# A spectral filter and MLP on one core: the remainder products of the last 64 features taken as 64-row products, two steps' side by side in TensorE's row halves

## The chip, the core and the metric

The kernel runs on one core of a Trainium2 chip. The core has TensorE (PE in the profile; its loads of stationary operands are shown apart, as PEld), VectorE (DVE), ScalarE (ACT), GpSimd (POOL) and SyncE (SP, which here issues nearly all DMAs). The metric is the device time of one execution in microseconds; before the change it is 1029.7 us, the median of three runs (1028.49 to 1030.01).

## The reference

Two residual blocks over 2048 tokens of 576 features, all in float32. The first is a spectral filter, the second an MLP with a ReLU between its two layers:

```python
h = x + irfft2(rfft2(layernorm(x)) * (w_r + 1j * w_i))
h2 = h + maximum(layernorm(h) @ w1, 0) @ w2      # w1: 576 x 4608, w2: 4608 x 576
```

## The kernel before

The program is one hand-ordered list of instructions for each engine; what is written first in the code runs first on its engine.

**Three stretches.** Up to about 100 us the tokens are normalized and transformed (lines 258 to 399). Then comes the inverse transform, in a loop `u` (line 739) which for two token tiles at a time also does the second normalization (`stat2`, `norm2`) and the transposition of the normalized tile (`project`, line 505), and which starts the first steps of the MLP (`unit`). From about 200 us on only the MLP runs.

**Two numbers for each.** Products run on data of the type float32r. Operands are split in two of that type, a high part (the rounded value, written by ScalarE) and a low part or remainder (value minus high part). A product of two matrices is three products: high by high, high by low, low by high.

**The MLP's steps.** The 4608 hidden features are taken in 18 groups `g` of 256, the tokens in four chunks `c` of 512; a step is one pair (g, c), 72 in all, listed in `steps` (line 727). From step 8 (`WINO`) on the order is group by group, chunks 0, 1, 2, 3 in each, so that neighbouring steps have neighbouring chunks, the last chunk of a group being followed by the first of the next.

**The transposed tokens.** `xc[c]` holds a chunk transposed: features on the 128 partitions, 512 tokens along the row, in nine blocks. Blocks 0 to 3 are the high parts of features 0 to 511, blocks 5 to 8 their low parts. Block 4 holds the last 64 features, 512 to 575, twice: on partitions 64 to 127 the high part, on partitions 0 to 63 the low part. `project` makes it: the last transpose (line 510) takes features 448 to 575, so that the last 64 land in the upper partitions; one ScalarE copy of 640 columns writes blocks 0 to 4 (line 514), another 512 plain columns for GpSimd's subtraction, and VectorE writes the low part into the lower half (line 520).

**The first layer** is `mm1(i, a, part)` (line 525): for step i and half a of its 256 hidden features, a sum over 14 products of 128 rows and 512 columns. Blocks 0 to 3 give three each; block 4 gives two, with the high weights (times high and low part at once, since the weights of the last 64 features are loaded in both partition halves) and with the low weights. From step 9 on the sum is cut in two parts of seven products; the four (a, part) are the step's quarters 0 to 3.

**The second layer** in those steps is a scheme with seven block products instead of eight (`prod`, line 620), each of six products of 288 columns. `slot(i)` (line 655) runs step i's seven block products and between them the four quarters of step i+1's first layer: quarter 0, A11·B11 and A12·B21, quarter 1, S2·T2 and S1·T1, quarter 2, S3·T3 and S4·B22, quarter 3, A22·T4. After quarters 1 and 3 ScalarE, VectorE and GpSimd take the ReLU, the splits and the sums of the hidden values (`hid_a`, line 607), which later block products read. The sums of the first layer lie in two PSUM tiles, one for each a, with one bank for even and one for odd steps (`hid_p`, line 604).

**Weights.** `load_weights` (line 306) loads a group's weights five steps ahead of its first step. `split_weights` (line 325) queues their split in pieces; for the first layer there are five, one for each block, and `work(1)` in the slots of chunks 1 and 2 takes the next piece from the queue: three in the slot of chunk 1, two in that of chunk 2.

Of the kernel before, what the change touches and what calls it, by code (L numbers as in the profile page):

```python
# [21 lines left out]
GF = 2  # L22
NG = DFF // (128 * GF)
CH = 4
# [104 lines left out]
def kernel(ctx: ExitStack, tc: tile.TileContext, x, w_r, w_i, w1, w2, cc2, c1, fb, ib, c3, out):  # L129
    nc = tc.nc  # L130
# [3 lines left out]
    def sb(shape, tag, bufs=1, dt=F32):  # L134
        n[0] += 1
        return pool.tile(shape, dt, tag=tag, name=f"{tag}_{n[0]}", bufs=bufs)
# [3 lines left out]
    def ps():  # L140
        n[0] += 1
        return psum.tile([128, 1024], F32, tag="d", name=f"d_{n[0]}", bufs=4)

    def ebuf(shape, dt=F32):
        e = sb([128, EW], "e", EB, dt)[:, :int(np.prod(shape[1:]))]
        return e.rearrange("p (a b) -> p a b", a=shape[1]) if len(shape) == 3 else e

    def mm(o, l, r, start, stop):
        nc.tensor.matmul(o, l, r, start=start, stop=stop)  # L149

    def act(o, i, **kw):
        nc.scalar.activation(o, i, AF.Copy, **kw)  # L152
# [9 lines left out]
    ident = sb([128, 128], "ident")  # L162
# [141 lines left out]
    raw, wts = {}, {}  # L304
# [16 lines left out]
    def work(k):  # L321
        for _ in range(k):
            split(*pieces.pop(0))

    def split_weights(g, part):
        if g == 1 and part == 0:
            h, l = tail[0][:, 4608:5888], tail[0][:, 5888:7168]
        else:
            h, l = (ebuf([128, (1280, 1152)[part]], F32R) for _ in range(2))
        h, l = (v.rearrange("p (a n) -> p a n", a=(5, 2)[part]) for v in (h, l))  # L330
        wts[g, part] = h, l
        for k in range((5, 2)[part]) if g >= 2 else [slice(None)]:
            pieces.append((h[:, k], l[:, k], raw[g][part][:, k]))
        if g <= 2:
            work(len(pieces))
# [63 lines left out]
    for i in range(NP + 2):  # L399
        if i < NP:  # L400
            if i % 2 == 0:
                mid_l(i, i + 1)
            mid_d(i)
        if i == NP - 3:
            load_weights(0)
        if 1 <= i <= NP:
            mid_b(i - 1)
        if i >= NP:
            split_weights(0, i - NP)
        if i >= 2:  # L410
            if i > NP:
                warm_pe(8)
            mid_i(i - 2)
# [16 lines left out]
    xc = [xc01[:, 0], xc01[:, 1], xc2]  # L430
# [74 lines left out]
    def project(t):  # L505
        y = Zs.pop(t)
        pz = ps()
        for b in range(4):
            nc.tensor.transpose(pz[:, 128 * b:128 * b + 128], y[:, 128 * b:128 * b + 128], ident)  # L509
        nc.tensor.transpose(pz[:, 512:640], y[:, 448:576], ident)  # L510
        q = slice(128 * (t % CH), 128 * (t % CH) + 128)
        dst = xc[t // CH]
        pzv = pz.rearrange("p (a s) -> p a s", s=128)
        act(dst[:, 0:5, q], pzv[:, :5])
        if t % 2 == 0:
            Ez[t] = ebuf([128, 1024])
        zt = Ez[t - t % 2][:, 512 * (t % 2):512 * (t % 2) + 512]
        act(zt, pz[:, :512])
        nc.gpsimd.tensor_sub(dst[:, 5:9, q], zt.rearrange("p (a s) -> p a s", s=128), dst[:, 0:4, q])
        nc.vector.tensor_sub(dst[0:64, 4, q], pzv[64:128, 4], dst[64:128, 4, q])  # L520

    hid = {}
    pend = {}

    def mm1(i, a, part=None):
        g, c = steps[i]
        w1h, w1l = wts[g, 0]
        if a == 0 and not part:
            pend[i] = None if i >= WINO else ps()
        p = hid_p(i, a) if i >= WINO else pend[i][:, 512 * a:512 * a + 512]  # L530
        f = slice(128 * a, 128 * a + 128)
        ops = []
        for kt in range(4):
            ops += [(w1h, kt, kt), (w1h, kt, 5 + kt), (w1l, kt, kt)]
        ops += [(w1h, 4, 4), (w1l, 4, 4)]
        for n_, (w, kt, xk) in enumerate(ops):
            if part is None or n_ // 7 == part:
                mm(p, w[:, kt, f], xc[c][:, xk, :], n_ == 0, n_ == len(ops) - 1)
        if i >= WINO:
            return  # L540
        if a == GF - 1:
            p = pend.pop(i).rearrange("p (a s) -> p a s", a=GF)
            hh, hl = sb([128, GF, 512], "D", 4, F32R), sb([128, GF, 512], "D", 4, F32R)
            nc.scalar.activation(hh, p, AF.Relu)  # L544
            nc.vector.scalar_tensor_tensor(hl, p, 0.0, hh, op0=ALU.max, op1=ALU.subtract)  # L545
            hid[i] = (hh, hl)
# [21 lines left out]
    WINO = 8  # L568
# [35 lines left out]
    def hid_p(i, k):  # L604
        return wps[2 + k][:, 512 * (i % 2):512 * (i % 2) + 512]
# [49 lines left out]
    def slot(i):  # L655
# [4 lines left out]
        def quarter(k):  # L660
            mm1(i + 1, k // 2, k % 2)
            if k % 2 and end:
                for hs in range(2):
                    relu_split(fs[f"A{hs + 1}{k // 2 + 1}"], hid_p(i + 1, k // 2)[:, 256 * hs:256 * hs + 256])
            elif k % 2:
                hid_a(i + 1, k // 2)
# [60 lines left out]
    steps = first + [(g, c) for g in range(2, NG) for c in range(NC)]  # L727

    def unit(k):
        i, q = divmod(k, 4)  # L730
        if q < 2:
            mm1(i, q)
        else:
            if i == 2:
                mm1(3, q - 2)
            mm2(i, 2 * q - 4)
            mm2(i, 2 * q - 3)

    for u in range(NT // 2 + 3):
        if u <= NT // 2:  # L740
            inv_h(u, u != 1)
        if 2 * u < NT:
            inv_d(2 * u)
            inv_d(2 * u + 1)
        if u == 1:
            inv_r(u)
        if u == 7:
            load_weights(1)
        if u == 8:
            tail.append(sb([128, 10240], "X", dt=F32R))  # L750
            xc.append(tail[0][:, :4608].rearrange("p (a n) -> p a n", a=9))
        if 3 <= u:
            project(2 * u - 6)
            project(2 * u - 5)
        if 1 <= u <= NT // 2:
            stat2(2 * u - 2)
            stat2(2 * u - 1)
        if 2 <= u < NT // 2 + 2:
            for _ in norm2(2 * u - 4, 2):
                pass  # L760
        if u in (8, 9):
            split_weights(1, u - 8)
        if 5 <= u:
            unit(2 * u - 10)
            unit(2 * u - 9)
    for i in range(3, len(steps)):
        if i + 5 < len(steps) and steps[i + 5] == (steps[i + 5][0], 0):
            load_weights(steps[i + 5][0])
        if i + 3 < len(steps) and steps[i + 3] == (steps[i + 3][0], 0):
            split_weights(steps[i + 3][0], 0)  # L770
        if i == WINO - 3:
            wino_sums(2, 1, 2, 3, 4)
        if i == WINO - 2:
            wino_w("B11", "B21", "T2", "T1", "T3")
        if i == WINO - 1:
            wps += [None, None, ps(), ps()]
            wino_tiles()
        if i == WINO:
            wps[:2] = ps(), ps()
        if i >= WINO:  # L780
            (slot if i + 1 < len(steps) else slot_last)(i)
            continue
        for a in range(GF):
            mm1(i + 1, a)
            if i == WINO - 1:
                hid_a(i + 1, a)
        for tt in range(CH):
            mm2(i, tt)
        if i == WINO - 1:
            relu_split(fs["A22"], hid_p(i + 1, 1)[:, 256:])  # L790
            split(*fs["S3f"], fs["S3"])
            wino_w("B22", "T4")
# [22 lines left out]
```

## Time and profile before

| | us |
|---|---|
| median of three runs | 1029.7 |
| span of the profiled execution | 1026.5 |
| PE busy | 1011.1 |
| DVE busy | 741.4 |
| ACT busy | 391.1 |
| POOL busy | 326.0 |

The profile shows one execution. Its span runs from the first to the last instruction; the 3.2 us between it and the median of the runs lie around it. A row of a timeline has the start, the length from the first start to the last end, the engine, the line, the operation, out<-in by the program's names with the buffer numbers left out, for a product the rows and columns of PE's array that it uses (128*128, 64*64), then partitions x elements of the operand, and the count; a bracket holds the idle time before it and who ended it. Neighbouring products overlap, since the end of one is modelled with the time that its result needs to come out: the time that one takes is read from start to start. The chain of waits is the work that ended last, followed backwards and listed in order of time.

### The profile page before, as it was taken

What the parts mean: (1) busy time and instruction counts of PE and PEld (TensorE: products, weight loads), DVE (VectorE), ACT (ScalarE), POOL (GpSimd) and SP (SyncE); (2) the same over time, 40 slices, a digit from 0 to 9 for tenths busy, and PEclk for the clock granted to TensorE, in tenths of its full rate; (3) what the DMA queues carried; (4) which work ended last, traced back from release to release, by engine and by line L of the source; (5) the groups of instructions that cost most, each with busy time, mean ns of one, the idle gap of its engine ahead of it and who ended that gap; (6) DMA issues with size and microseconds to landing.
All of it is one profiled execution on the core that took longest, in us unless ns stands there. A gap on an engine that the chain in (4) does not pass through costs nothing.

```text
span 1026.5 us, 17863 instructions
## 1 busy us (share of the span) xinstructions
PE 1011.1 (98%) x6894; PEld 899.2 (88%) x6894; DVE 741.4 (72%) x1366; ACT 391.1 (38%) x891; POOL 326.0 (32%) x429
## 2 busy tenths in 40 slices
PE   7999999999999999999999999999999999999997
PEld 6877678899999999999999999999999999999997
DVE  7689877334678777777777777877777777777774
ACT  5645354311233343343334343334334333334331
POOL 4201465110233333323232433333332323243321
PEclk7999999999999999999999999999999999999999
DMA  9944500110000000000110000000000011000024
GB/s 243 219 129 115 121 21 30 49 38 13 27 24 27 25 27 24 27 24 27 33 41 27 24 27 24 27 24 26 24 27 24 26 33 41 27 24 1 1 59 127
DMA packets 32101, 48.01 MB, mean 47 GB/s; under 512 B 2960, under 2 KB 22800, under 8 KB 32016
## 3 DMA queue, kind: packets, MB, share of 16 engines
q1 hardware_dynamic: 31280, 45.98, 16.7%
q8 instruction: 55, 0.90, 0.4%
q10 hardware_dynamic: 736, 0.89, 0.3%
q14 instruction: 30, 0.25, 0.1%
HBM read 42.13 MB, written 4.72 MB: 46 GB/s over the span
## 4 chain that ended last, share of the span: by engine, by line
PE 94%; DVE 3%; DMA 2%; SPq 0%; ACT 0%; issue 0%; DVEq 0%; ACTq 0%
PE d L149 58%; PE d L627 35%; DMA A<-in_A_x_dram 2%; DVE st L209 1%; PE d L509 1%; DMA X<-in_A_x_dram 0%; DVE A L469 0%; DVE D L545 0%; DVE e L253 0%; DVE mv L210 0%; ACT D L544 0%; DVE e L252 0%; DVE e L488 0%; SPq L424 0%; SPq L160 0%
## 5 line engine op out<-in xcount | busy, mean ns | idle before, releaser
L634 DVE TENSOR_TENSOR A<-A,d 128x576 f32<-128x576 f32 x445 | 332.5, 747 | 51.2 <-PE d L627 51.0
L627 PE MATMUL d<-X,D 128*128 128x288 f32 x2286 | 342.8, 294 | 0.0
L627 PEld LDWEIGHTS d<-X,D 128*128 128x128 f32 x2286 | 326.4, 188 | 14.7
L149 PE MATMUL d<-B,e 128*128 128x512 f32 x952 | 237.4, 390 | 0.0
L149 PEld LDWEIGHTS d<-B,e 128*128 128x128 f32 x952 | 171.9, 188 | 27.9 <-issue 0.2
L602 DVE SCALAR_TENSOR_TENSOR D<-d,D 128x256 fp32r<-128x256 f32 x191 | 81.1, 425 | 121.8 <-ACT D L601 121.8
L601 ACT ACTIVATE D<-d 128x256 fp32r<-128x256 f32 x191 | 73.0, 382 | 242.3 <-PE d L149 242.3
L616 POOL TENSOR_TENSOR e<-e 128x256 f32<-128x256 f32 x63 | 46.6, 740 | 350.0 <-ACT e L615 350.0
L149 PE MATMUL d<-C,e 128*128 128x512 f32 x476 | 119.0, 390 | 0.0
L149 PE MATMUL d<-X,e 128*128 128x512 f32 x476 | 118.8, 390 | 0.0
L152 ACT ACTIVATE X<-e 128x288 fp32r<-128x288 f32 (+2 forms) x176 | 69.8, 434 | 103.5 <-PE d L627 103.5
L317 DVE TENSOR_TENSOR D<-e,D 128x512 fp32r<-128x512 f32 x126 | 91.2, 724 | 19.5 <-ACT D L152 19.5
L612 POOL TENSOR_TENSOR e<-e 128x256 f32<-128x256 f32 x63 | 46.8, 744 | 170.1 <-ACT e L611 170.1
L149 PEld LDWEIGHTS d<-C,e 128*128 128x128 f32 x476 | 85.9, 188 | 13.8
L149 PEld LDWEIGHTS d<-X,e 128*128 128x128 f32 x476 | 85.9, 188 | 13.7
L152 ACT ACTIVATE D<-e 128x512 fp32r<-128x512 f32 x126 | 65.6, 521 | 73.7 <-POOL e L617 70.2
L317 DVE TENSOR_TENSOR X<-e,X 128x288 fp32r<-128x288 f32 (+2 forms) x176 | 82.8, 493 | 0.3 <-POOL r L212 0.3
L627 PEld LDWEIGHTS d<-X 128*128 128x128 f32 x378 | 57.2, 188 | 4.9
L627 PE MATMUL d<-X 128*128 128x288 f32 x378 | 60.4, 295 | 0.0
L149 PE MATMUL d<-e,D 128*128 128x288 f32 x384 | 52.7, 296 | 0.0
L149 PEld LDWEIGHTS d<-e,D 128*128 128x128 f32 x384 | 51.9, 189 | 0.7 <-ACT e L152 0.2
L617 POOL TENSOR_TENSOR e<-e,e 128x256 f32<-128x256 f32 x63 | 49.7, 790 | 4.9
(86 smaller groups left out, 938.0 us busy)
## 6 DMA issues: line engine op xcount, KB each, us to landing
e<-in_B_w_dram SPq DMA_DIRECT2D x18, 576.0 KB, 4.0
e<-in_B_w_dram SPq DMA_DIRECT2D x18, 512.0 KB, 3.7
A<-in_A_x_dram SPq DMA_DIRECT2D x16, 288.0 KB, 8.7
out_dram<-A SPq DMA_DIRECT2D x28, 144.0 KB, 2.5
X<-in_A_x_dram SPq DMA_DIRECT2D x12, 288.0 KB, 7.4
e<-in_B_w_dram SPq DMA_DIRECT2D x36, 64.0 KB, 3.5
B<-in_A_w_r_dram SPq DMA_DIRECT2D x15, 144.5 KB, 7.5
B<-in_A_w_i_dram SPq DMA_DIRECT2D x15, 144.5 KB, 7.1
```

The source lines that it names most:

```text
L149: nc.tensor.matmul(o, l, r, start=start, stop=stop)
L152: nc.scalar.activation(o, i, AF.Copy, **kw)
L209: nc.vector.bn_stats(st[:, i, h, :], xs[:, t0 + i, 288 * h:288 * h + 288])
L317: eng.tensor_sub(l, v, h)
L509: nc.tensor.transpose(pz[:, 128 * b:128 * b + 128], y[:, 128 * b:128 * b + 128], ident)
L601: nc.scalar.activation(h, p, AF.Relu)
L602: nc.vector.scalar_tensor_tensor(l, p, 0.0, h, op0=ALU.max, op1=ALU.subtract)
L612: nc.gpsimd.tensor_sub(fs["S3"], fs["p0"][:, 0], fs["p0"][:, 1])
L616: nc.gpsimd.tensor_add(fs["S1"], fs["p0"][:, 1], fs["p1"][:, 1])
L617: nc.gpsimd.tensor_sub(fs["S2"], fs["S1"], fs["p0"][:, 0])
L627: nc.tensor.matmul(P[:, tt], l[:, q], r, start=first and n_ == 0, stop=end and n_ == 2, skip_group_check=whole and not first)
L634: nc.vector.tensor_add(xt, xt, P)
```

## The change

The product of block 4 with the low weights now takes only the 64 rows with the high part of the tokens; the product of low weights and low part is left out. For this the high part lies in the upper partitions in even chunks (as before) and in the lower ones in odd chunks. The 64-row product of step i, half 1, is the last of quarter 3, and right behind it stands the one of step i+1, half 0, as the first product of that sum, with another row half and another bank. So from step 9 on the sum of half 0 has this product ahead of the other 13. Steps 0 to 7 keep their 14 products, and so does half 0 of step 8; the last step's half 1 has its 64-row product alone.

For odd chunks the last transpose takes 64 features in place of 128, and the copy of blocks 0 to 4 becomes two, one of 64 partitions by 128 columns and one of 512 columns. The five weight pieces are split in another order, block 4 first, since its low weights are now read two quarters earlier.

```diff
-        for k in range((5, 2)[part]) if g >= 2 else [slice(None)]:
+        for k in ((4, 0, 1, 2, 3), (0, 1))[part] if g >= 2 else [slice(None)]:
             pieces.append((h[:, k], l[:, k], raw[g][part][:, k]))
...
-        nc.tensor.transpose(pz[:, 512:640], y[:, 448:576], ident)
+        up = t // CH % 2 == 0
+        nc.tensor.transpose(pz[slice(0, 128 if up else 64), 512:640], y[:, 448:576] if up else y[:, 512:576], ident)
...
-        act(dst[:, 0:5, q], pzv[:, :5])
+        if up:
+            act(dst[:, 0:5, q], pzv[:, :5])
+        else:
+            act(dst[0:64, 4, q], pzv[0:64, 4])
+            act(dst[:, 0:4, q], pzv[:, :4])
...
-        nc.vector.tensor_sub(dst[0:64, 4, q], pzv[64:128, 4], dst[64:128, 4, q])
+        hi, lo = (slice(64, 128), slice(0, 64)) if up else (slice(0, 64), slice(64, 128))
+        nc.vector.tensor_sub(dst[lo, 4, q], pzv[hi, 4], dst[hi, 4, q])
...
+    lead = set()
+
+    def rest_low(i, a, start):
+        g, c = steps[i]
+        q = slice(0, 64) if c % 2 else slice(64, 128)
+        nc.tensor.matmul(hid_p(i, a), wts[g, 0][1][q, 4, 128 * a:128 * a + 128], xc[c][q, 4, :], start=start, stop=not start)
...
-        ops += [(w1h, 4, 4), (w1l, 4, 4)]
+        ops += [(w1h, 4, 4)]
+        ahead = (i, a) in lead
+        apart = i >= WINO and a == GF - 1
+        if not ahead and not apart:
+            ops += [(w1l, 4, 4)]
         for n_, (w, kt, xk) in enumerate(ops):
             if part is None or n_ // 7 == part:
-                mm(p, w[:, kt, f], xc[c][:, xk, :], n_ == 0, n_ == len(ops) - 1)
+                mm(p, w[:, kt, f], xc[c][:, xk, :], n_ == 0 and not ahead, n_ == len(ops) - 1 and not apart)
+        if apart and part != 0:
+            rest_low(i, a, False)
+            if i + 1 < len(steps):
+                rest_low(i + 1, 0, True)
+                lead.add((i + 1, 0))
```

## The prediction

> **What bounds the kernel now.** I read the page first, then a window over the long stretch of the multilayer part, the chain of waits, and the timeline of one step.
>
> ```profile
> PE 1011.1 (98%) x6894; PEld 899.2 (88%) x6894; DVE 741.4 (72%) x1366; ACT 391.1 (38%) x891; POOL 326.0 (32%) x429
> ...
> PE 94%; DVE 3%; DMA 2%; SPq 0%; ACT 0%; issue 0%; DVEq 0%; ACTq 0%
> ```
>
> TensorE (PE) is 94% of the chain that ends last. The window from 207 to 1014 us gives busy time by engine, then the granted clock (1.00):
>
> ```profile
> 207.00:1014.00 807.00, 807.00 (x4757) 733.03 (x4756) 588.64 (x1036) 293.31 (x703) 256.65 (x317) 1.00 0.09 27
> ```
>
> PE is busy in all 807 us; VectorE, the next, in 588.64 (73%). So in the steps from 8 on, time on PE counts one to one. Their length stands in the chain, listed in order of time:
>
> ```profile
> 848.06 1.60 PE d L149 x7
> 859.98 1.60 PE d L149 x7
> ...
> 1002.93 1.60 PE d L149 x7
> 1014.05 7.16 PE d L627 x54
> ```
>
> From 848.06 to 1002.93 are 13 steps, so 11.91 us each. One step in the timeline (start, length, engine):
>
> ```profile
> 500.03 1.75 PE L149 MATMUL d<-B,e 128*128 128x512 f32 x7
> ...
> 501.62 0.96 PE L627 MATMUL d<-X,D 128*128 128x288 f32 x6
> ...
> 502.29 1.46 PEld L149 LDWEIGHTS d<-B,e 128*128 128x128 f32 x7
> ...
> 502.41 1.76 PE L149 MATMUL d<-B,e 128*128 128x512 f32 x7
> ...
> 504.01 1.75 PE L627 MATMUL d<-X,D 128*128 128x288 f32 x12
> ...
> 505.12 0.63 ACT L152 ACTIVATE D<-e 128x512 fp32r<-128x512 f32 x1 [0.83 <-POOL e L617]
> ...
> 505.59 1.75 PE L149 MATMUL d<-B,e 128*128 128x512 f32 x7
> ...
> 505.99 0.68 DVE L317 TENSOR_TENSOR D<-e,D 128x512 fp32r<-128x512 f32 x1
> ...
> 507.18 1.75 PE L627 MATMUL d<-X,D 128*128 128x288 f32 x12
> ```
>
> Seven first-layer products take 507.18 - 505.59 = 1.59, so 0.227 each; twelve of 288 columns take 505.59 - 504.01 = 1.58, so 0.132 each. 28 x 0.227 + 42 x 0.132 = 11.90: the step is these products and nothing else. The reader should also see PEld at 502.29, ahead of its products at 502.41: the weights of the next product load while the one before it runs, so the loads cost nothing.
>
> **The main edit.** Steps 8 to 71 (64 of them) lose the last product of quarter 3, and steps 9 to 71 (63) lose the last of quarter 1: 127 products, 0.454 us per step. What comes in are 63 pairs of 64-row products and one single one (step 71). Each stands after the sixth product of quarter 3 and ahead of A22·T4, between products that use all 128 rows. So every pair changes PE's shape twice: 128*128 to 64*128 and back.
>
> Price of the change in. The only like place with a 512-column product ahead is at 143.78; the rows are the PE and PEld timelines there:
>
> ```profile
> 143.78 0.39 PE L149 MATMUL d<-B,e 128*128 128x512 f32 x1
> 144.10 0.47 PE L149 MATMUL d<-e,X 64*64 64x290 f32 x4
> 144.40 0.42 PE L149 MATMUL d<-e,X 64*64 64x290 f32 x4
> 144.64 0.42 PE L149 MATMUL d<-e,X 64*64 64x290 f32 x4
> ...
> 144.10 0.15 PEld L149 LDWEIGHTS d<-e,X 64*64 64x64 f32 x4 [0.35 <-issue]
> ```
>
> The next product starts 0.32 after the 512-column one in place of 0.227: 0.09 lost. And its weights were not loaded ahead: PEld was idle for 0.35 and starts with the product. The first group of four lasts 0.30, the second 0.24: 0.06 for a load of 64 columns laid bare. For 128 columns the forward transform shows it, pairs of 64-row products of the very shape 64*128:
>
> ```profile
> 31.13 0.39 PE L149 MATMUL d<-cc,e 64*128 64x128 f32 x2
> 31.35 0.40 PE L149 MATMUL d<-cc,e 64*128 64x128 f32 x4
> 31.58 0.40 PE L149 MATMUL d<-cc,e 64*128 64x128 f32 x4
> ```
>
> 31.13 is the first pair after a change of shape: 0.22 to the next pair, while the two pairs from 31.35 take 0.23, 0.115 each. So 0.105 laid bare, and the change in costs 0.09 + 0.105 = 0.195.
>
> Price of the change out:
>
> ```profile
> 147.32 0.41 PE L149 MATMUL d<-X,cc 64*64 64x288 f32 x3
> 147.67 0.39 PE L149 MATMUL d<-e,X 128*128 128x145 f32 x1
> 147.90 0.41 PE L149 MATMUL d<-e,X 128*128 128x145 f32 x2
> 148.02 0.41 PE L149 MATMUL d<-e,X 128*128 128x145 f32 x2
> ```
>
> The last 64*64 group starts at 147.32 and would be followed after 0.24 (its kind at 144.40); it is followed after 0.35. That is 0.11; rows to the hundredth and a record missing from the group (x3) leave 0.09 to 0.11, and I take 0.09, as at the change in. The first full product then lasts 0.23 to the next, the second 0.12: 0.11 laid bare. Out: 0.20.
>
> Both places change rows and columns together. That rows alone do the same is shown at 64 columns:
>
> ```profile
> 44.63 0.42 PE L149 MATMUL d<-e,A 64*64 64x290 f32 x4
> 44.98 0.34 PE L149 MATMUL d<-e,A 128*64 128x145 f32 x2
> ```
>
> Again 0.35 from group to group. That rows alone do it at 128 columns no row shows; I take it. The Trainium skill, "TensorEngine Tiling (Array Packing)", Key Properties, speaks for it: changing the tiling mode, as against the tile, empties the array first. Without that rule the sum would be that of the last rival.
>
> Price of the pair itself. Of the pairs from 31.35 each takes 0.115, a single 128-row product of that width 0.108 (the transposes below): two row halves run together, and the second adds 0.007. But these stream 128 columns in 0.11, against 512 in 0.227 here; a pair at the new rate is not shown. Bounds: 0.234 (together: 0.227 + 0.007) and 0.454 (one after the other). I take 0.234, for every group of row halves in these rows runs together. The Trainium skill, "TensorE: Matmul & The Clock Gate", Part 3, gives a measured 3.07 times for four row tiles of 512 columns; by that 77% the pair would be an estimated 0.30, and the sum some 4 us more; no row here shows it.
>
> Sum per step: 0.234 + 0.195 + 0.20 - 0.454 = +0.175; with the load at 0.06 in place of 0.105 it would be 0.13. Times 63: +11.0. The single one at the end pays both changes, +0.39, but replaces a product of its length: +0.4.
>
> **Who waits for the moved products.** The ReLU of quarter 3 now waits for the pair's first member: last full product + 0.32 + 0.49, before + 0.227 + 0.39, so 0.195 later. Its chain ends in the split of S12f (505.12, then 505.99 to 506.67), due at 507.18: 0.51 to spare. PE comes there 0.40 (the pair) - 0.227 (quarter 1 is one shorter) = 0.17 later, so 0.02 of the 0.51 goes. No new wait. The pair's second member writes the half bank whose reader ran a step earlier. It reads piece 4 of the remainder weights two quarters earlier than the product that it replaces; that piece is now split first of the five, a step (11.91) ahead of this use. No DMA moves and SP's order is the same.
>
> **The transposes.** Token tiles 4 to 7 and 12 to 15 end in a 64-column transpose; their stretch:
>
> ```profile
> 136.34 0.60 PE L509 MATMUL d<-ident,e 128*128 128x128 f32 x4
> 136.77 0.27 PE L510 MATMUL d<-ident,e 128*128 128x128 f32 x1
> 136.88 0.60 PE L509 MATMUL d<-ident,e 128*128 128x128 f32 x4
> ...
> 137.54 6.63 PE L149 MATMUL d<-B,e 128*128 128x512 f32 x28
> ...
> 98.56 0.22 PE L149 MATMUL d<-D,e 128*64 128x64 f32 x1
> 98.72 0.33 PE L286 MATMUL d<-ident 128*128 128x128 f32 x1
> 98.88 0.38 PE L286 MATMUL d<-ident 128*128 128x128 f32 x2
> ```
>
> Five transposes take 0.54, 0.108 each. A change of columns alone costs too: the 64-column product at 98.56 is followed after 0.16, and the transpose after it lasts 0.16 in place of 0.108, 0.05 laid bare. The 64-column transpose still streams 128 columns, so 0.09 + 0.03 to 0.05 in, and 0.09 + 0.05 (next a transpose) or + 0.10 (next a product) out: 0.27 or 0.32, four of each: +2.4. PE is the chain here too; bounds 1.0 (half hidden in its short waits) and 3.1 (the dearer load everywhere). The eight tiles also cost ScalarE a copy of 64 x 128 more each:
>
> ```profile
> 137.08 0.70 ACT L152 ACTIVATE B<-d 128x640 fp32r<-128x640 f32 x1
> ...
> 144.21 1.02 ACT L544 ACTIVATE D<-d 128x1024 fp32r<-128x1024 f32 x1 [3.34 <-PE d L149]
> ```
>
> It lies between 0.14 (0.70 by its share of the 640 columns) and 0.70, and falls ahead of 3.34 us in which ScalarE stands idle: nothing. Without that cover it would be, at an estimated 0.3 each, 2.4.
>
> **Sum.** 11.0 + 0.4 + 2.4 = +13.8 on a span of 1026.5, so 1040.3. The median of the runs, 1029.7, lies 3.2 above that span, which stays: 1043.5.
>
> **The rivals.**
> - The pair runs one member after the other. For it: no row shows two streams at the full rate. Against: the rows from 31.35, at half the rate. 0.22 x 63 = 13.9 more: 1057.4. Chance 0.08.
> - The weights load ahead across the change of shape, so that only the 0.09s are paid: 0.234 + 0.18 - 0.454 = -0.04 a step, -2.5; the single one +0.2; transposes 8 x 0.18 = +1.4: 1028.8, within 0.2%. Against: PEld idle until 144.10. The Trainium skill, "TensorE: Matmul & The Clock Gate", Part 2 (step 1), would have it so, since it lets loads pass products in flight when row groups don't conflict or the background buffer is meant; the trace has it within one shape only. Chance 0.05.
> - Not slower: 64*128 after 128*128 is no change of shape to the array. Then every pair is 0.234 for 0.454, -0.22 x 63 = -13.9, and the transposes (a column change, shown) keep +2.4: 1018.2. It decides from the first pair. For it: this very change is in no row that isn't idle; against it 44.98. Chance 0.07.
>
> **How the numbers follow.** The forecast keeps 0.80; time 1043.5. Its own range by its terms: -3 (the load's lower bound), -1.4 (transposes half hidden); +0.7 (transposes), +1.5 (0.11 for both loads and 0.11 for the drain out), and up to a quarter of the serial rival (3.5). So 1038 to 1049, which also leaves out no more than the three rivals, 0.20. About 0.2% (2 us) is what a measurement of this kernel can tell from none: slower 0.88, same 0.05, faster 0.07.
>
> **What would show it.** Steps of 12.09 us in the chain; a 64*128 row about 0.32 after the sixth product, its mate 7 ns on, A22·T4's first product 0.42 to 0.43 after the mate and its second 0.23 after the first; PE still without idle time. Steps of 11.7 would prove the third rival, 12.3 the first. The forecast is wrong if the 64*128 row stands 0.227 behind, or if PE shows a wait at A22·T4.

## The result and the profile after

The changed kernel takes 1042.78 us (median of four runs, 1041.81 to 1043.19) against 1029.1 for the one before (four runs): a ratio of 1.0133, 95% interval 1.0119 to 1.0148, so 13.7 us slower. The span of the profiled execution is 1039.9 us, against 1026.5.

The page of the changed kernel, engines and chain:

```profile
PE 1024.3 (98%) x6894; PEld 882.9 (85%) x6894; DVE 763.2 (73%) x1366; ACT 391.4 (38%) x899; POOL 322.4 (31%) x429
...
PE 94%; DMA 2%; DVE 2%; ACT 0%; issue 0%; SPq 0%; ACTq 0%; DVEq 0%
PE d L149 55%; PE d L648 36%; PE d L535 3%; DMA A<-in_A_x_dram 2%; DMA X<-in_A_x_dram 1%; DVE st L209 1%; PE d L509 1%; DVE A L469 0%; DVE D L566 0%; DVE mv L210 0%; ACT D L565 0%; DVE e L488 0%; SPq L424 0%; DVE e L487 0%; DVE X L491 0%
```

PE has 13.2 us more and is still 94% of the chain; L535, the 64-row products, is new in it. VectorE has 21.8 us more, though it has no more instructions; this comes back below. The chain in order of time (start, length), eight steps apart:

```profile
925.32 1.61 PE d L149 x7
...
1022.25 1.62 PE d L149 x7
1027.26 7.34 PE d L648 x54
```

96.93 / 8 = 12.12 us a step in place of 11.91. Around one pair, in the timeline (start, length, engine, and in brackets the idle time before):

```profile
952.51 1.53 PE L149 MATMUL d<-B,e 128*128 128x512 f32 x6
...
953.97 0.18 PEld L535 LDWEIGHTS d<-B,e 64*128 64x128 f32 x1 [0.35 <-issue]
953.97 0.50 PE L535 MATMUL d<-B,e 64*128 64x512 f32 x1
...
953.97 0.50 PE L535 MATMUL d<-C,e 64*128 64x512 f32 x1
954.40 0.83 PEld L648 LDWEIGHTS d<-X,D 128*128 128x128 f32 x6 [0.24 <-issue]
954.40 1.06 PE L648 MATMUL d<-X,D 128*128 128x288 f32 x6
...
955.30 1.77 PE L149 MATMUL d<-C,e 128*128 128x512 f32 x7
```

The two members start in the same hundredth of a microsecond: they run side by side. On both sides PEld stands idle (0.35 and 0.24) and begins its load together with the product that needs it. The six products and the six of A22·T4 alone would take 6 x 0.227 + 6 x 0.132 = 2.15; here 955.30 - 952.51 = 2.79 pass from the start of the first to the next quarter. The 0.64 between is the price of the pair with its changes of shape. It replaces two products of 0.227, 0.454 together: 0.19 more in this step.

### The profile page after: what moved, and what is told of

Its sections match the earlier page's. It is cut to its first block, busy times and chain, and to the rows that moved or that the text cites. A ratio compares the mean times of both kernels' runs of the same rounds, so it can differ in the third digit from the quotient of the medians.

```text
span 1039.9 us, 17871 instructions
## 1 busy us (share of the span) xinstructions
PE 1024.3 (98%) x6894; PEld 882.9 (85%) x6894; DVE 763.2 (73%) x1366; ACT 391.4 (38%) x899; POOL 322.4 (31%) x429
## 4 chain that ended last, share of the span: by engine, by line
PE 94%; DMA 2%; DVE 2%; ACT 0%; issue 0%; SPq 0%; ACTq 0%; DVEq 0%
PE d L149 55%; PE d L648 36%; PE d L535 3%; DMA A<-in_A_x_dram 2%; DMA X<-in_A_x_dram 1%; DVE st L209 1%; PE d L509 1%; DVE A L469 0%; DVE D L566 0%; DVE mv L210 0%; ACT D L565 0%; DVE e L488 0%; SPq L424 0%; DVE e L487 0%; DVE X L491 0%
## 5 line engine op out<-in xcount | busy, mean ns | idle before, releaser
L655 DVE TENSOR_TENSOR A<-A,d 128x576 f32<-128x576 f32 x445 | 332.9, 748 | 69.1 <-PE d L648 63.4
L648 PE MATMUL d<-X,D 128*128 128x288 f32 x2286 | 351.2, 298 | 0.0
L648 PEld LDWEIGHTS d<-X,D 128*128 128x128 f32 x2286 | 322.6, 188 | 25.6 <-issue 15.0
L149 PE MATMUL d<-B,e 128*128 128x512 f32 x889 | 223.2, 390 | 0.0
L149 PEld LDWEIGHTS d<-B,e 128*128 128x128 f32 x889 | 160.1, 188 | 25.5 <-issue 0.2
L317 DVE TENSOR_TENSOR D<-e,D 128x512 fp32r<-128x512 f32 x126 | 109.9, 872 | 19.1 <-ACT D L152 19.1
L149 PE MATMUL d<-C,e 128*128 128x512 f32 x444 | 112.2, 391 | 0.0
L149 PE MATMUL d<-X,e 128*128 128x512 f32 x444 | 111.9, 390 | 0.0
L152 ACT ACTIVATE X<-e 128x288 fp32r<-128x288 f32 (+2 forms) x176 | 69.8, 435 | 105.2 <-PE d L648 105.2
L152 ACT ACTIVATE D<-e 128x512 fp32r<-128x512 f32 x126 | 65.6, 521 | 73.7 <-POOL e L638 70.0
L149 PEld LDWEIGHTS d<-C,e 128*128 128x128 f32 x444 | 79.8, 188 | 13.1
L149 PEld LDWEIGHTS d<-X,e 128*128 128x128 f32 x444 | 79.9, 188 | 12.7
L317 DVE TENSOR_TENSOR X<-e,X 128x288 fp32r<-128x288 f32 (+2 forms) x176 | 82.7, 493 | 0.3 <-POOL r L212 0.3
```

Source lines behind the costliest of these rows:

```text
L317: eng.tensor_sub(l, v, h)
L648: nc.tensor.matmul(P[:, tt], l[:, q], r, start=first and n_ == 0, stop=end and n_ == 2, skip_group_check=whole and not first)
L655: nc.vector.tensor_add(xt, xt, P)
```

## The experiments

All ratios are against the kernel before, in the same session.

**The layout alone.** All sums as before; only the tokens' layout, the transposes, the extra copy and the order of the weight pieces are changed.

```diff
-        ops += [(w1h, 4, 4)]
...
-        if not ahead and not apart:
-            ops += [(w1l, 4, 4)]
+        ops += [(w1h, 4, 4), (w1l, 4, 4)]
...
-        if apart and part != 0:
-            rest_low(i, a, False)
...
```

> The change's layout alone: odd chunks with the high part in the lower partitions, their 64-column transposes and the extra copy, and the new order of the weight pieces; all first-layer sums have 14 products of 128 rows again. By the step of the prediction, eight 64-column transposes cost 0.27 or 0.32 us each: about +2.4 us, so 1031.5. By the trace of the changed kernel, where these transposes start 0.109 us apart like the others, they cost nothing: 1029.1, within 0.2%.

Measured: 1028.62, ratio 0.9999 (0.9990 to 1.0008). To within the 1 us of the interval all of it is free, the transposes too. Their rows in this run's timeline of PE:

```profile
136.13 0.60 PE L509 MATMUL d<-ident,e 128*128 128x128 f32 x4
136.57 0.27 PE L511 MATMUL d<-ident,e 128*64 128x128 f32 x1
136.68 0.60 PE L509 MATMUL d<-ident,e 128*128 128x128 f32 x4
137.11 0.27 PE L511 MATMUL d<-ident,e 128*64 128x128 f32 x1
137.33 2.97 PE L149 MATMUL d<-B,e 128*128 128x512 f32 x12
```

136.13 to 136.68 is 0.55 for five transposes, 0.11 each, as before; the shape reads 128*64, but there is no gap on either side of it among the transposes. The 0.22 from the last one to the products at 137.33 stand in the kernel before too (137.32 to 137.54).

**Both moved products with 128 rows.** The sums are in the change's order, and the two products stand where the pair does, but they use all rows (and so add the low weights times the low part, as before the change).

```diff
-        q = slice(0, 64) if c % 2 else slice(64, 128)
+        q = slice(0, 128)
```

> The change with both moved products taken with all 128 rows (low weights times high and low part): same place, same order, no change of the array's shape. If the changes of shape are the cost, the steps fall back to 11.91 us and the time to 1029 (up to 1032 if GpSimd's sums still start ahead of VectorE's split in the slots of chunks 1 and 2). If the move itself costs (the later ReLU, the sum that opens a step early), most of the 13.7 us stays: about 1040.

Measured: 1030.66, ratio 1.0020 (1.0011 to 1.0029). So 11.7 of the 13.7 us go with the 64-row shape: the changes into it and out of it, less what the pair saves. 2.0 stay, which the move alone costs; below it is shown from what.

**Both members in one row half.** In odd chunks this multiplies the low part of the tokens in place of the high part.

```diff
-        q = slice(0, 64) if c % 2 else slice(64, 128)
+        q = slice(64, 128)
```

> The change with both 64-row products of a pair in the upper row half (in odd chunks this multiplies the low part of the tokens in place of the high part). Still two changes of shape a step. If the two row halves of the change really run side by side, the second member now takes a turn of its own, 0.22 us a step: 12.34 us a step, 1042.8 + 14 = 1057. If they ran one after the other all along and only the records start together, nothing changes: 1043.

Measured: 1054.77, ratio 1.0255 (1.0241 to 1.0269). The chain of this run:

```profile
935.94 1.59 PE d L149 x7
...
1034.44 1.59 PE d L149 x7
1039.40 7.38 PE d L648 x54
```

98.50 / 8 = 12.31 a step: 0.22 more than the 12.09 of a step of the change in which nothing else stalls (the run with later sums, below). That is one product's time for one member more in turn, so in the change the row halves do run side by side at the full rate. The time rose by some 12 us over the change, not by 14: the stall that the move brings isn't in these steps, which are all 12.31 or 12.32, though VectorE's splits are slowed in this run too (821 ns on its page, 724 before; see below). Presumably that is because PE comes 0.22 later to the place at which it stalled.

**Each 64-row product alone.** No pair; each is the last of its own sum, so a step has four changes of shape.

```diff
-        apart = i >= WINO and a == GF - 1
+        apart = i >= WINO
...
-            if i + 1 < len(steps):
-                rest_low(i + 1, 0, True)
-                lead.add((i + 1, 0))
```

> Each 64-row product alone as the last of its own sum, at the end of quarters 1 and 3: four changes of shape a step and no pair. If every way there and back costs 0.39 us, a step has 2 x 0.39 = 0.78 us more than before: 12.69 us, times 63.5 about +49.5, so 1078.6. If the price is the pair's or a wait of VectorE's and not the shape's, the steps stay under 12.2 us: 1045 or less.

Measured: 1079.64, ratio 1.0500 (1.0485 to 1.0514). Its chain:

```profile
951.10 1.60 PE d L149 x7
...
1052.78 1.60 PE d L149 x7
1059.54 1.60 PE d L149 x7
1064.51 7.34 PE d L645 x54
```

101.68 / 8 = 12.71 a step, 0.80 over before, so 0.40 for every way into the shape and out of it. Here too all steps are alike, without that stall. The price scales with the number of changes, as expected.

**What the move costs.** The slot beside GpSimd's weight sums, first in the kernel before, then in the changed one; the rows are ScalarE's and VectorE's halves of the S12f split (L152, L317), VectorE's add of A11·B11 ahead of it (L634, L655), and GpSimd's sums (L584, L605):

```profile
957.71 0.75 DVE L634 TENSOR_TENSOR A<-A,d 128x576 f32<-128x576 f32 x1 [0.56 <-PE d L627]
957.79 0.63 ACT L152 ACTIVATE D<-e 128x512 fp32r<-128x512 f32 x1 [1.15 <-POOL e L617]
...
958.45 0.69 DVE L317 TENSOR_TENSOR D<-e,D 128x512 fp32r<-128x512 f32 x1
958.53 2.16 POOL L584 TENSOR_TENSOR e<-e,e 128x288 f32<-128x288 f32 x2
959.06 0.75 DVE L634 TENSOR_TENSOR A<-A,d 128x576 f32<-128x576 f32 x1
...
959.89 1.75 PE L627 MATMUL d<-X,D 128*128 128x288 f32 x12
...
961.47 0.62 PE L149 MATMUL d<-X,e 128*128 128x512 f32 x2
```

```profile
957.76 0.63 ACT L152 ACTIVATE D<-e 128x512 fp32r<-128x512 f32 x1 [1.15 <-POOL e L638]
...
957.91 0.76 DVE L655 TENSOR_TENSOR A<-A,d 128x576 f32<-128x576 f32 x1 [0.77 <-PE d L648]
...
958.52 2.01 POOL L605 TENSOR_TENSOR e<-e 128x288 f32<-128x288 f32 x2
958.58 1.29 DVE L317 TENSOR_TENSOR D<-e,D 128x512 fp32r<-128x512 f32 x1
959.79 0.74 DVE L655 TENSOR_TENSOR A<-A,d 128x576 f32<-128x576 f32 x1
959.86 1.79 PE L648 MATMUL d<-X,D 128*128 128x288 f32 x12
...
961.49 1.79 PE L149 MATMUL d<-C,e 128*128 128x512 f32 x7
```

Count from ScalarE's half, which ends the ReLU's chain. The sums start 0.74 and 0.76 behind it, unmoved, since they hang on the same chain. VectorE's half stands in its queue behind the add of A11·B11, and that waits for PE (the bracket). PE now comes there later against the ReLU: the add starts 0.15 behind ScalarE's half where it started 0.08 ahead, and the split 0.82 behind in place of 0.66. So the sums now start first, and the split takes 1.29 in place of 0.69. Behind it stands the next add (959.79 to 960.53), for whose PSUM bank S1·T1 waits with its weight load: that load would start with the product before it, at 960.52, and starts at 960.58, behind the add's end. The twelve products from 959.86 take 1.63 in place of 1.58 (959.89 to 961.47).

The Trainium skill, "SBUF — State Buffer", section "SBUF: two separate sides", states that a VectorE operation with two SBUF inputs and a GpSimd operation that reads SBUF share a port pair: whichever starts first holds it for the whole instruction, and the other waits. The traces agree both ways. With the split first, it takes 0.69 and the first of the two sums 1.28; with the sum first, the sum takes 0.80 and the split 1.29.

To test it, the sums are issued behind quarter 1, so that GpSimd has S3 to do first:

```diff
-        if w1:
-            wino_sums(g + 1, *((1, 3) if c == 1 else (2, 4)))
...
         quarter(1)
+        if w1:
+            wino_sums(g + 1, *((1, 3) if c == 1 else (2, 4)))
```

> The change, with GpSimd's two weight sums of the slots of chunks 1 and 2 issued behind quarter 1 in place of ahead of it, so that they follow GpSimd's S3 and cannot stand beside VectorE's split of S12f. If the stall of S1 T1 in these slots comes from that split (1.29 us beside the sums, 0.69 without), their steps fall from 12.15 to 12.08 us and the time by 62 x 0.041 = 2.6 to about 1039.8. If the stall has another cause (the later ReLU, PE's own restart after a change of shape), it stays at 1042.5.

Measured: 1040.62, ratio 1.0118 (1.0104 to 1.0131). That is 1.5 us less by the two ratios where 2.6 were expected. The interval overlaps the change's own, so the time alone doesn't settle it; the rows do. This run's group of splits on its page (count, busy, mean ns), and its chain:

```profile
L317 DVE TENSOR_TENSOR D<-e,D 128x512 fp32r<-128x512 f32 x126 | 91.5, 726 | 19.1 <-ACT D L152 19.1
```

```profile
923.58 1.59 PE d L149 x7
...
1020.30 1.59 PE d L149 x7
1025.26 7.34 PE d L648 x54
```

The mean split is back at 726 ns (the change: 872, before: 724), and the step is 96.72 / 8 = 12.09 in place of 12.12. The group holds two shapes, and only one of them changed: the 63 splits of S12f take 687 ns on average before, 986 in the change and 692 here, while the 63 of 128x256 stay at some 760. So the splits of S12f are 63 x 0.299 = 18.8 of the 21.8 us that VectorE had more in the change.

**The same with 128 rows.** Both edits together: products of 128 rows, sums behind quarter 1.

> The moved products with all 128 rows and GpSimd's sums behind quarter 1. By the same reason the 2.0 us that the move cost without any change of shape vanish: 1028.7, within 0.2% of before. If the move costs by itself, it stays at 1030.7.

Measured: 1028.97, ratio 1.0004 (0.9996 to 1.0013). Most or all of the 2.0 us is gone (the two intervals share only 1.0011 to 1.0013). The group of splits, first on the page of the run with 128 rows and the sums ahead of quarter 1, then on this run's:

```profile
L317 DVE TENSOR_TENSOR D<-e,D 128x512 fp32r<-128x512 f32 x126 | 109.2, 867 | 19.2 <-ACT D L152 19.2
```

```profile
L317 DVE TENSOR_TENSOR D<-e,D 128x512 fp32r<-128x512 f32 x126 | 91.5, 726 | 19.1 <-ACT D L152 19.1
```

867 ns falls to 726 (977 to 691 for S12f alone). So GpSimd's sums beside the split are the price of the move, as far as these runs can tell.

**Four products at one place.** To pay the changes of shape once in two steps, all four 64-row products of an even step and the next stand at the end of quarter 1, as two pairs.

```diff
-        apart = i >= WINO and a == GF - 1
+        apart = i >= WINO and i % 2 == 0 and a == 0
...
-            rest_low(i, a, False)
-            if i + 1 < len(steps):
-                rest_low(i + 1, 0, True)
-                lead.add((i + 1, 0))
+            rest_low(i, 0, False)
+            for s in ((i + 1, 0), (i, 1), (i + 1, 1)):
+                rest_low(*s, True)
+                lead.add(s)
```

> All four 64-row products of two neighbouring steps at one place, the end of quarter 1 of the even step: two pairs, one way into the shape and back for two steps. By the measured terms two steps pay 0.092 + 0.428 + 0.100 + 0.235 = 0.855 us for four products of 0.227 = 0.910: -0.05 us in two steps, less what the restart behind the change of shape takes (0.01 to 0.02): about -1.3 us, 1027.4. The move between the ReLU of quarter 3 and A11 B11 is undone, so VectorE's split should keep its place ahead of GpSimd's sums. If a second pair cannot load its weights behind the first, it costs 0.1 us more for two steps: 1030.5.

Measured: 1028.65, ratio 1.0002 (0.9993 to 1.0011): the same as before, not 1.3 us faster. PE's timeline:

```profile
946.30 1.53 PE L149 MATMUL d<-C,e 128*128 128x512 f32 x6
947.75 0.50 PE L535 MATMUL d<-C,e 64*128 64x512 f32 x1
947.76 0.50 PE L535 MATMUL d<-X,e 64*128 64x512 f32 x1
948.09 0.39 PE L535 MATMUL d<-C,e 64*128 64x512 f32 x1
948.10 0.39 PE L535 MATMUL d<-X,e 64*128 64x512 f32 x1
948.42 1.88 PE L648 MATMUL d<-X,D 128*128 128x288 f32 x12
950.14 1.09 PE L149 MATMUL d<-C,e 128*128 128x512 f32 x4
```

The second pair loads its weights behind the first (its products last 0.39, not 0.50), so that reason falls. But the twelve products behind the change of shape take 1.72 in place of 1.58: 0.14, where 0.10 was counted and 0.01 to 0.02 for the restart. That, with a little in the next quarter, eats the 0.05. Why PE takes some 0.04 longer to settle is open.

**The transposes as plain products.** The layout alone, with the eight 64-column transposes written as products with the identity.

```diff
-        nc.tensor.transpose(pz[slice(0, 128 if up else 64), 512:640], y[:, 448:576] if up else y[:, 512:576], ident)
+        if up:
+            nc.tensor.transpose(pz[:, 512:640], y[:, 448:576], ident)
+        else:
+            mm(pz[0:64, 512:640], y[:, 512:576], ident, True, True)
```

> The layout alone (as in the run of that name), but the 64-column transposes of the odd chunks are plain products with the identity matrix. If 64 columns in themselves need no change of the array's shape, these eight start 0.11 us after the transpose before them, as the transposes do, and the time stays at 1028.6. If it was the transposing that spared the change, they start 0.20 us after it, as the prediction took from the 64-column products of the spectral part, and the eight cost 2.2 to 2.6 us: 1031.

Measured: 1032.52, ratio 1.0042 (1.0028 to 1.0055). PE's timeline of this run:

```profile
136.32 0.60 PE L509 MATMUL d<-ident,e 128*128 128x128 f32 x4
136.85 0.43 PE L149 MATMUL d<-ident,e 128*64 128x128 f32 x2
137.21 0.66 PE L509 MATMUL d<-ident,e 128*128 128x128 f32 x4
```

The fourth transpose starts 0.60 - 0.27 = 0.33 after 136.32, at 136.65; the plain product follows after 0.20, the transpose in its place (136.57, in the rows of the layout alone) after 0.11. So these 64 columns cost a gap as a plain product, and the transposing spares it. The rise is more than the 2.2 to 2.6 us expected, and a part of it is something else: a plain product shows two records (x2), a transpose one, and the second adds 0.43 - 0.27 = 0.16, eight times 1.3 us. A plain product behind a transpose needn't wait: in the layout alone one of 128 columns in float32r starts at 150.52, right behind the 64-column transpose at 150.50. But the product with the identity is in plain float32, and no run has one of those with 128 columns there, so that the gap comes from its 64 columns and not from its type is likely and not shown. The Trainium skill, "TensorEngine Tiling (Array Packing)", Gotcha 2, has a rule that fits: column tiling excludes the transpose mode with FP32 input. By it the 128*64 of a transpose's row isn't the smaller array, and the missing gap agrees.

## Why the prediction came out, step by step

The forecast was 1043.5, the result 1042.78. The main mechanism was right in kind and size. Two smaller steps were wrong, and their errors nearly cancel, which is luck.

- **Changes of shape and the pair: right.** "Sum per step: 0.234 + 0.195 + 0.20 - 0.454 = +0.175." An undisturbed step (sums behind quarter 1) is 12.09, +0.17 to +0.18. Four changes a step cost 0.80, two 0.41 (the 0.64 around the pair less 0.234), as the sum of 0.195 and 0.20 says; 128 rows at the same place cost none of it. That rows alone change the shape at 128 columns was assumed; the 0.35 at 953.97 shows it.
- **The pair side by side: right.** Both members start at 953.97, and in one row half a step takes 0.22 more. The 0.64 less 0.195 and 0.20 leave 0.245 for the pair, near the 0.234 taken, not the 0.30 that the prediction estimated beside it.
- **"No new wait": wrong.** The working let the split of S12f move with the ReLU. In VectorE's queue it stands behind the add of A11·B11, which moves with PE; the split so lost its place ahead of GpSimd's sums. In the runs that cost 2.0 us without the change of shape. Of the 0.51 to spare nothing is left in these slots: the split ends at 959.87, and the products that it feeds begin at 959.86. The traces had it: the split began 0.08 ahead of the sums.
- **The transposes: wrong, +2.4 predicted, 0 measured.** The step took the row at 98.56, a plain product with 64 columns, for the price of a transpose with 64. The layout alone is free, and with plain products it isn't.
- **ScalarE's copies and the order of the pieces at nothing: right.** The layout alone holds both.
- **The rivals.** The serial pair falls with the run in one row half. Loads that run ahead across the change of shape fall with the idle PEld on both sides of the pair. A free change of shape falls with the result and with the run of single products.

In sum: 11.0 + 0.4 + 2.4 = 13.8 were put together, and 13.7 were found: 11.7 for all changes of shape and 2.0 from another place than the third term's. The single product of the last step is in the 11.7 with its 0.4: from the start of its quarter to the end of the twelve products behind it 3.58 us pass (1025.30 to 1028.88), before the change 3.17 (1012.30 to 1015.47).

The base moved a little as well. The forecast stood on a median of 1029.7 from three runs, which a fourth made 1029.1. And the 3.2 us between span and median don't all lie around the span: in each of the changed kernel's four runs 1.9 do. Its median lies 2.9 above the profiled span because the profiled run (1041.81) was the fastest of the four.

## What to carry to other kernels

A product on half the rows saves only when it shares a change of shape with enough others: here the way in and out costs 0.40 us, so one pair saves 0.22 and loses 0.40, and two pairs, which should have gained a little, only break even. When an instruction is moved on the busiest engine, ask for each queue what stands behind an instruction that follows it: an 0.08 us lead of VectorE over GpSimd was worth 2 us. A row's shape doesn't say which mode ran; take the price from a row of the same operation.

## What was not expected of the hardware

An operation of VectorE that starts 0.06 us behind one of GpSimd took 1.29 us in place of 0.69. A transpose with 64 columns runs among transposes of 128 with no gap (0.11 from start to start), a plain float32 product of that size has 0.20 ahead of it. After a change of shape the next twelve products took 0.14 more, of which the bare weight load is 0.10.
